# Retention, ELU block and gated block on one core: a first pass in 256-token groups, score banks of their own, earlier loads, and a lag of two

## The chip, the cores and the metric

The kernel runs on one core of a Trainium2 chip. Its engines each have a queue of their own and run in order: PE multiplies matrices into PSUM, DVE (VectorE) and ACT (ScalarE) work on PSUM and SBUF, POOL (GpSimd) works on SBUF alone, and SP (SyncE) issues the transfers. They wait for one another by semaphores. The metric is the device time of one execution in microseconds (us), the median of several runs. The profile is of one execution; PE has two clock levels, 1.2 and 2.4 GHz, and the profile gives the granted one as a share of 2.4 GHz.

## The reference

Three parts follow one another over 2304 tokens (4 batches of 576) with 512 features.

```python
scores = scale * np.matmul(q, k.transpose(0, 1, 3, 2))      # 4 batches, 8 heads, 576 tokens, 64 wide
ret = scores * Dmat                                         # gamma ** (i - j) where i >= j, else 0
attn_out = np.matmul(ret, v)
x = attn_out.transpose(0, 2, 1, 3).reshape(B * S, H * D)    # 2304 x 512
h = x @ w_in                                                # 512 -> 2048
g = np.where(h > 0.0, h, np.exp(np.minimum(h, 0.0)) - 1.0)
x = g @ w_out                                               # 2048 -> 512
gate = 1.0 / (1.0 + np.exp(-(x @ w_gate)))                  # 512 -> 1536
out = gate * (x @ w_val) @ w_out2                           # 1536 -> 512
```

## The kernel before

**Retention** is done in 18 *steps*. A step takes 64 tokens of two batches (X = 0, 1) and all heads, so 128 tokens of the output. `scores` writes K^T Q of the step into PSUM (64x64 matmuls in fp32, each of which stands twice in the trace) and DVE masks it into `a` with `tri` (L192). `outs` is 48 such matmuls (96 in the trace), in three parts: state times Q (32 in the trace, reading `st`), K V for the new state (32), and `a` times V (32). Then DVE adds the new state to `st` (L219); in every second step POOL scales `st` (L222); DVE scales the output out of PSUM (L228, twice); ACT and DVE split it into a high and a low part of `x` (L81, L82). Ahead of a step, POOL scales its V in place (`scale`, L176). All of this uses one PSUM tile `T` of two banks: scores and the new state share its lower half-banks, the outputs its upper ones.

The three parts of `outs` use different rows of the PE array for the same banks. So that the second doesn't overtake the first, the program puts a `nop` on SP that waits for the first 16 matmuls and for which the K V matmuls wait. It stands in SP's queue among the transfers. The transfers (L165 for q and k of two batches and two steps, L169 for k and v of one step, L105 for a weight) share eight semaphores in turn, so each is issued only after the eighth before it has landed, and after the tile it writes has been read for the last time. Steps are loaded two ahead.

**The two dense blocks** take the tokens in five groups, four of 512 and one of 256 (`GS`), and the hidden features in *passes* of two blocks of 128 (`FP`): 8 passes of the ELU block (0 to 7), then 6 of the gated block. A *unit* is one group and one block of features. `up` makes h (12 matmuls: 4 blocks of features times 3, since a product of split numbers is hi·hi + hi·lo + lo·hi); the activation on ACT and DVE gives `e`; ACT and POOL split it into `g` (L81, L82); `down` multiplies `g` by the second weight (12 matmuls) into four PSUM banks `acc`, over both units of a group; `evac` then adds them to `y` (DVE L266). In pass 7 it also splits y for the gated block, on ACT and POOL. The units run with a lag of one: PE does `up` of unit s, then `down` of unit s - 1.

A weight is 512 KB of 64-bit numbers and is turned into two fp32r parts by a *chain* of ACT, DVE and POOL work (L114 to L123, then L81 and L82), which the program spreads over a unit. Four or six chains run in each pass for the next one. The weights of passes 2 and 5 and most of those of passes 8, 10 and 12 lie in a second pool (`w2`), made when the retention's tiles are given up.

Everything is written in the order in which the engines run it. At the start come 18 warm-up matmuls, then 5 steps (`AHEAD`) with the chains of the first four weights between them, then pass 0, in which `retention()` is called ahead of each half of `up` and of `down` and runs half a step each time:

```python
                    retention()
                    up(x_of[g], W["i", f].w, h, (0, 1))
                    first_half()
                    retention()
```

Of the kernel before, what the change touches and what calls it, by code (L numbers as in the profile page):

```python
# [19 lines left out]
NP = H // 2  # L20
# [14 lines left out]
AHEAD = 5  # L35
WARM = 18
# [7 lines left out]
def retention_elu_glu(  # L44
# [22 lines left out]
    ps_acc = ctx.enter_context(tc.tile_pool(name="ps_acc", bufs=4, space=bass.MemoryType.PSUM))  # L67
    ps_h = ctx.enter_context(tc.tile_pool(name="ps_h", bufs=2, space=bass.MemoryType.PSUM))
    ps_t = ctx.enter_context(tc.tile_pool(name="ps_t", bufs=1, space=bass.MemoryType.PSUM))

    acc_bank = lambda: ps_acc.tile([128, 512], F32, tag="acc", name="acc")
# [5 lines left out]
    T = ps_t.tile([128, 2, 512], F32, name="t")  # L77
# [6 lines left out]
    def mm3(out_, wh, wl, xh, xl, start, stop):  # L84

        pe.matmul(out_, wh, xh, start=start, stop=False)  # L86
        pe.matmul(out_, wh, xl, start=False, stop=False)  # L87
        pe.matmul(out_, wl, xh, start=False, stop=stop)  # L88
# [10 lines left out]
    class Weight:  # L99
# [3 lines left out]
        def load(self):  # L103
            self.raw = rpool.tile([128, 2 * DM], I32, tag="raw", name="raw")
            sp.dma_start(out=self.raw, in_=self.src.bitcast(I32))  # L105
# [40 lines left out]
    x_of, y_of, acc, g_of = {}, {}, {}, {}  # L146

    class Step:
# [4 lines left out]
        def __init__(self, n):  # L153
# [4 lines left out]
            self.at = 128 * (n - G0[self.g])  # L158

        def load(self):  # L160
            key = (self.b, self.c)
            if key not in Step.qk:
                Step.qk[key] = [qkpool.tile([128, NP, 2 * C], F32, tag=f"qk{X}", name=f"qk{X}") for X in range(2)]
                for X in range(2):
                    sp.dma_start(out=Step.qk[key][X],  # L165
                                 in_=ain[self.b + X, self.c, :, :, : 2 * C].rearrange("p q x -> q p x"))
            self.kv = kvpool.tile([128, NP, 2 * C], F32, tag="kv", name="kv")
# [5 lines left out]
        def scale(self):  # L173
            v = self.kv[:, :, C:].rearrange("t p (h d) -> t p h d", h=2)
            by = vt[self.s].rearrange("t (p x) -> t p x", x=4)[:, :, 2:4].unsqueeze(3).to_broadcast([128, NP, 2, D])
            pool.tensor_tensor(out=v, in0=v, in1=by, op=ALU.mult)  # L176
# [4 lines left out]
        def scores(self):  # L181
            s = slice(HC * self.s, HC * self.s + HC)
            ks = slice(C + HC * self.s, C + HC * self.s + HC)
            qk = Step.qk[self.b, self.c]
# [119 lines left out]
    with tc.manual_schedule():  # L304
# [38 lines left out]
        def retention():  # L343
# [3 lines left out]
            if n >= NSTEP:  # L347
                return
# [180 lines left out]
```

## Time and profile before

| | us |
|---|---|
| median of 3 runs (lowest, highest) | 973.81 (972.59, 974.82) |
| the profiled execution | 977.69 |
| its span, first to last instruction | 975.6 |
| PE busy | 924.0 |
| DVE, ACT, POOL busy | 458.4, 360.8, 331.0 |

A matmul's end is modelled, so busy PE time overlaps; how fast PE goes is read from the distance of two starts. What a stage costs is read from stretches cut where a pass begins.

### The profile page before, as it was taken

How to read it: one execution, taken by the hardware profiler on the slowest of the kernel's cores; microseconds unless marked ns; L12 is line 12 of the kernel's file. 1: busy time of each engine (PE TensorE's matmuls, PEld its weight loads, DVE VectorE, ACT ScalarE, POOL GpSimd, SP SyncE). 2: the span in 40 equal slices, each digit the busy share in tenths (PEclk: the TensorE clock that was granted, in tenths of full speed). 3: DMA queues.
4: the chain of work that ended last, by engine and by line, in shares of the span. 5: the costliest groups of instructions: out<-in, count | busy, mean ns of one | idle time of the engine just before them, and what ended most of it. 6: DMA issues, size and time to landing. Idle time of an engine off the chain costs nothing.

```text
span 975.6 us, 15096 instructions
## 1 busy us (share of the span) xinstructions
PE 924.0 (95%) x6266; PEld 765.0 (78%) x6266; DVE 458.4 (47%) x740; ACT 360.8 (37%) x633; POOL 331.0 (34%) x261
## 2 busy tenths in 40 slices
PE   5578899999999999999989999999999999999997
PEld 4456778888888887888767888888888888888886
DVE  2554453454555555545666244355355354353222
ACT  1123346454544444444575234223223223222111
POOL 1424333343333334333676222233232232322111
PEclk8689999999999999999998999999999999999999
DMA  7466641110101111111121111111111110100124
GB/s 230 136 180 175 186 153 44 44 44 27 46 36 44 44 44 44 44 44 44 44 64 44 44 44 44 44 44 44 43 44 37 50 44 27 54 7 1 44 48 103
DMA packets 33859, 61.58 MB, mean 63 GB/s; under 512 B 3200, under 2 KB 22656, under 8 KB 33792
## 3 DMA queue, kind: packets, MB, share of 16 engines
q1 hardware_dynamic: 33792, 60.63, 21.0%
q8 instruction: 49, 0.80, 0.4%
q14 instruction: 18, 0.15, 0.0%
HBM read 55.90 MB, written 4.72 MB: 62 GB/s over the span
## 4 chain that ended last, share of the span: by engine, by line
PE 79%; DVE 6%; ACT 5%; POOL 3%; issue 2%; DMA 2%; SPq 0%; DVEq 0%; ACTq 0%; POOLq 0%
PE acc L87 10%; PE h L86 10%; PE h L88 10%; PE acc L88 10%; PE h L87 10%; PE acc L86 10%; PE t L86 5%; PE t L87 5%; PE t L88 5%; PE t L179 4%; POOL g L82 3%; DVE e L244 2%; DMA kv<-in_ain 2%; ACT e L242 1%; ACT e L241 1%
## 5 line engine op out<-in xcount | busy, mean ns | idle before, releaser
L82 POOL TENSOR_TENSOR g<-e,g 128x512 fp32r<-128x512 f32 (+1 forms) x140 | 189.4, 1353 | 549.8 <-ACT g L81 526.4
L86 PE MATMUL h<-x,w 128*128 128x512 f32 (+1 forms) x560 | 209.3, 374 | 0.0
L87 PE MATMUL h<-x,w 128*128 128x512 f32 (+1 forms) x560 | 207.7, 371 | 0.0
L88 PE MATMUL h<-x,w 128*128 128x512 f32 (+1 forms) x560 | 207.7, 371 | 0.0
L81 ACT CAST g<-e 128x512 fp32r<-128x512 f32 (+1 forms) x140 | 81.0, 579 | 220.1 <-DVE e L279 155.2
L279 DVE TENSOR_TENSOR e<-e,t 128x512 f32<-128x512 f32 (+1 forms) x60 | 38.1, 634 | 242.5 <-PE t L88 242.5
L87 PE MATMUL acc<-g,w 128*128 128x512 f32 (+1 forms) x320 | 121.3, 379 | 7.4 <-POOL g L82 7.4
L244 DVE SCALAR_TENSOR_TENSOR e<-e,h 128x512 f32<-128x512 f32 (+1 forms) x80 | 50.7, 633 | 154.9 <-ACT e L242 154.9
L86 PE MATMUL acc<-g,w 128*128 128x512 f32 (+1 forms) x320 | 120.7, 377 | 0.8 <-ACT g L81 0.8
L86 PEld LDWEIGHTS h<-x,w 128*128 128x128 f32 x560 | 105.8, 189 | 19.6
L88 PEld LDWEIGHTS h<-x,w 128*128 128x128 f32 x560 | 105.9, 189 | 18.9
L87 PEld LDWEIGHTS h<-x,w 128*128 128x128 f32 x560 | 105.9, 189 | 18.7
L88 PE MATMUL acc<-g,w 128*128 128x512 f32 (+1 forms) x320 | 119.3, 373 | 0.0
L82 POOL TENSOR_TENSOR w<-t,w 128x512 fp32r<-128x512 f32 x68 | 90.4, 1329 | 21.0 <-ACT w L81 20.9
L86 PE MATMUL t<-x,w 128*128 128x512 f32 (+1 forms) x240 | 88.7, 370 | 0.0
L87 PE MATMUL t<-x,w 128*128 128x512 f32 (+1 forms) x240 | 88.7, 370 | 0.0
L88 PE MATMUL t<-x,w 128*128 128x512 f32 (+1 forms) x240 | 88.5, 369 | 0.0
L274 ACT ACTIVATE e<-h 128x512 f32<-128x512 f32 (+1 forms) x60 | 33.3, 555 | 142.5 <-PE h L88 142.5
L86 PE MATMUL acc<-w,g 128*128 128x512 f32 x216 | 84.6, 392 | 0.0
L88 PE MATMUL acc<-w,g 128*128 128x512 f32 x216 | 84.6, 392 | 0.0
L87 PE MATMUL acc<-w,g 128*128 128x512 f32 x216 | 84.6, 391 | 0.0
L241 ACT ACTIVATE e<-h 128x512 f32<-128x512 f32 (+1 forms) x80 | 44.3, 554 | 99.8 <-PE h L88 97.4
(50 smaller groups left out, 1240.2 us busy)
## 6 DMA issues: line engine op xcount, KB each, us to landing
qk<-in_ain SPq DMA_DIRECT2D x20, 512.0 KB, 7.0
kv<-in_ain SPq DMA_DIRECT2D x36, 256.0 KB, 5.6
raw<-in_w_in SPq DMA_DIRECT2D x16, 512.0 KB, 3.6
raw<-in_w_out SPq DMA_DIRECT2D x16, 512.0 KB, 3.6
raw<-in_w_gate SPq DMA_DIRECT2D x12, 512.0 KB, 3.5
raw<-in_w_val SPq DMA_DIRECT2D x12, 512.0 KB, 3.5
raw<-in_w_o SPq DMA_DIRECT2D x12, 512.0 KB, 3.5
out<-y SPq DMA_DIRECT2D x36, 128.0 KB, 2.4
```

Source lines behind the costliest of these rows:

```text
L81: act.copy(hi, src)
L82: lo_engine.tensor_tensor(out=lo, in0=src, in1=hi.bitcast(F32), op=ALU.subtract)
L86: pe.matmul(out_, wh, xh, start=start, stop=False)
L87: pe.matmul(out_, wh, xl, start=False, stop=False)
L88: pe.matmul(out_, wl, xh, start=False, stop=stop)
L179: return pe.matmul(out_, w, x, start=start, stop=True, skip_group_check=True)
L241: act.activation(out=e, in_=h, func=AF.Relu, scale=-1.0)
L242: act.activation(out=e, in_=e, func=AF.Exp, scale=-1.0)
L244: dve.scalar_tensor_tensor(out=e, in0=e, scalar=-1.0, in1=h, op0=ALU.add, op1=ALU.max)
L274: act.activation(out=e, in_=h, func=AF.Sigmoid)
L279: dve.tensor_tensor(out=e, in0=e, in1=v, op=ALU.mult)
```

## The change

- Pass 0 takes the tokens in nine groups of 256 (`N0`), so it has 18 units with matmuls of 256 columns. Their four sums share two banks (`acc0`, `acc1`).
- Scores get a tile `ts` of two banks, outputs and new state another, `to`. `block(n)` issues the `outs` of step n, then the loads, then the scores of step n + 1 in one stretch; then the state, the scaling (one DVE instruction for both X), the mask and the split. One block goes ahead of each unit of pass 0; two (`AHEAD`) and the first scores go ahead of unit 0. The first step of a batch pair multiplies no state and copies the new one.
- Loads run five steps ahead. The additional tiles are the `y` tiles of later groups, as long as they are not written.
- The constants are loaded from ACT's queue. At the start, the chains of the first two weights follow the blocks whole instead of in pieces.
- `down` of unit s - 2 (`LAG`) follows `up` of unit s; `g` has four tiles instead of three, and a raw weight two instead of three. `evac` comes after all of `down` rather than after each half.
- In pass 7 half of the low parts of the split of y are made on DVE.

```diff
-AHEAD = 5
-WARM = 18
+N0 = 256
+AHEAD = 2
+LAG = 2
+WARM = 24
...
-    rpool = ctx.enter_context(tc.tile_pool(name="raw", bufs=3))
+    rpool = ctx.enter_context(tc.tile_pool(name="raw", bufs=2))
...
-    gpool = ctx.enter_context(tc.tile_pool(name="g", bufs=3))
+    gpool = ctx.enter_context(tc.tile_pool(name="g", bufs=LAG + 2))
...
+            if self.final:
                 x = x_of["b", g]
-                split(x[:, 0, e, :], x[:, 1, e, :], y, pool)
...
+                split(x[:, 0, e, :], x[:, 1, e, :], y, dve if e % 2 else pool)
...
+        for m in range(5, NSTEP):
+            loads_at.setdefault(m - 2 if m == NSTEP - 1 else m - 5, []).append(steps[m].load_kv)
...
+        def block(n):
+
+            if n >= 0:
                 steps[n].outs()
-                if n + 2 < NSTEP:
-                    steps[n + 2].load()
...
+            for load in loads_at.get(n, []):
+                load()
+            if n + 1 < NSTEP:
+                steps[n + 1].scores()
+            if n >= 0:
+                steps[n].state()
+                steps[n].x_scaled()
+            if n + 1 < NSTEP:
+                steps[n + 1].causal()
+            if n + 2 < NSTEP:
+                steps[n + 2].scale()
+            if n >= 0:
+                steps[n].x_low()
...
+        block(-1)
+        for n in range(AHEAD):
+            block(n)
+            for _ in weights[2 * n].chain():
+                pass
...
+        ff = [FF("a", 0, j // 2, f, passes[0][1], j % 2 * N0, N0) for j in range(NT // N0) for f in passes[0][1]]
...
+            if s < begins[1] and s + AHEAD < NSTEP:
+                block(s + AHEAD)
+            if s < len(ff):
+                ff[s].ups(stage, s)
...
+            if s >= LAG:
+                ff[s - LAG].downs(stage)
```

**Where it moves instructions.** Three places matter below. The first is PE within pass 0. Before, six dense matmuls of 512 columns stand between the last matmuls of `outs` (read from `kv` and `a`) and the scores of the next step:

```order
511 L179 MATMUL t<-kv 64x64 x16
512 L179 MATMUL t<-a,kv 64x64 x16
513 L86 MATMUL acc<-g,w 128x512
514 L87 MATMUL acc<-g,w 128x512
515 L88 MATMUL acc<-g,w 128x512
...
519 L179 MATMUL t<-qk_1454 64x64 x2
520 L179 MATMUL t<-qk_1455 64x64 x2
```

After, the scores follow at once, and then a whole unit of 256 columns (12 matmuls of `up`, 12 of `down`) stands ahead of the next step:

```order
585 L189 MATMUL to<-y_110 64x64 x16
586 L189 MATMUL to<-a,y_110 64x64 x16
587 L189 MATMUL ts<-qk_1513 64x64 x2
588 L189 MATMUL ts<-qk_1514 64x64 x2
...
595 L84 MATMUL h<-x_114,w 128x256
596 L85 MATMUL h<-x_114,w 128x256
```

The second is SP's queue at the start. Before, q and k (`qk`), `kv` and weights of the first steps, with eight transfers of constants among them:

```order
3 L169 DMA kv<-in_ain 64x4x256 x2
4 L328 DMA vt_102<-in_csmall 64x16 x2
5 L328 DMA vt_103<-in_csmall 64x16 x2
6 L331 DMA tri<-in_csmall 64x64 x2
7 L332 DMA cq_sb<-in_cq 128x512
8 L333 DMA cs_sb<-in_csmall 128x20
9 L105 DMA raw<-in_w_in 128x1024
10 L169 DMA kv<-in_ain 64x4x256 x2
```

After, twenty transfers of steps 0 to 4 and of four weights stand there (rows 1 to 14; `y_107` to `y_110` are the borrowed tiles), and row 15 is the load of step 5, which follows `outs` of step 0; the `nop` of step 1 (not printed) comes behind row 15, that of step 2 behind row 18:

```order
11 L179 DMA y_109<-in_ain 64x4x256 x2
12 L103 DMA y_107<-in_w_out 128x1024
13 L168 DMA y_108<-in_ain 128x4x256 x2
14 L179 DMA y_110<-in_ain 64x4x256 x2
15 L179 DMA kv<-in_ain 64x4x256 x2
16 L168 DMA qk_313<-in_ain 128x4x256
17 L168 DMA qk_314<-in_ain 128x4x256
18 L179 DMA kv<-in_ain 64x4x256 x2
```

The third is PE at the short group of a later pass (here pass 1). Before, `down` behind the short `up` (`h_2327`) reads `g_2303`, which is made from the h of the unit just before it (`h_2284`):

```order
L88 MATMUL h_2284<-x3_109,w_1795 128x512
L86 MATMUL acc_2310<-g_2262,w_1199 128x512
...
L86 MATMUL h_2327<-x4_110,w_814 128x256
...
L86 MATMUL acc_2310<-g_2303,w_1917 128x512
L87 MATMUL acc_2310<-g_2303,w_1917 128x512
```

After, `down` at that place reads `g_2460`, made one unit earlier than `h_2486`, whose own g is read only a unit later:

```order
L86 MATMUL h_2486<-x3_114,w_1580 128x512
L84 MATMUL acc_2465<-g_2418,w_2033 128x512
...
L84 MATMUL h_2525<-x4_115,w_804 128x256
...
L84 MATMUL acc_2549<-g_2460,w_1138 128x512
L85 MATMUL acc_2549<-g_2460,w_1138 128x512
```

## Rows read from the trace of the kernel before

**Rows 1.** Busy time, clock and DMA of six stages (stretch, length, engines, clock share, DMA share, GB/s).

```profile
0.00:53.22 53.22, 27.96 (x690) 24.72 (x690) 23.34 (x41) 10.84 (x17) 13.60 (x16) 0.72 0.65 191
53.22:157.78 104.56, 91.08 (x1801) 73.00 (x1797) 50.83 (x91) 39.64 (x71) 38.04 (x34) 0.96 0.56 155
157.78:463.26 305.48, 302.34 (x1443) 250.25 (x1441) 157.90 (x273) 146.48 (x256) 111.98 (x84) 1.00 0.13 42
463.26:521.32 58.06, 53.45 (x243) 43.38 (x241) 39.37 (x55) 36.23 (x64) 40.05 (x31) 0.94 0.18 55
521.32:970.13 448.81, 448.81 (x2102) 373.64 (x2100) 185.91 (x283) 127.61 (x225) 127.34 (x97) 1.00 0.14 42
970.13:975.58 5.45, 0.39 (x2) 0.00 (x0) 1.10 (x2) 0.00 (x0) 0.00 (x0) 0.74 0.42 96
```

**Rows 2.** PE's waits up to 53.2 us (in total, times, longest).

```profile
PE t L179 <- DVE a L192: 13.9, 5, 5.4
```

**Rows 3.** Transfers by kind (count, KB each, median us to landing).

```profile
qk<-in_ain SPq DMA_DIRECT2D x20, 512.0 KB, 7.0
kv<-in_ain SPq DMA_DIRECT2D x36, 256.0 KB, 5.6
raw<-in_w_in SPq DMA_DIRECT2D x16, 512.0 KB, 3.6
```

**Rows 4.** Two stretches with the transfer engines nearly full, columns as in rows 1.

```profile
10.00:22.50 12.50, 7.28 (x214) 7.04 (x218) 4.92 (x10) 3.59 (x6) 1.05 (x1) 0.78 0.99 292
65.00:80.00 15.00, 9.66 (x206) 7.70 (x208) 7.20 (x13) 4.04 (x7) 5.76 (x5) 0.95 0.96 242
```

**Rows 5.** PE's timeline in pass 0 around the scores (start, length).

```profile
102.01 0.39 PE L88 MATMUL h<-x,w 128*128 128x512 f32 x1
102.38 0.69 PE L179 MATMUL t<-qk 64*64 64x64 f32 x32
103.00 0.50 PE L86 MATMUL acc<-g,w 128*128 128x512 f32 x1
```

**Rows 6.** The chain that ended last, at `outs` of one step (start, us).

```profile
105.51 2.08 PE t L179 x94
```

**Rows 7.** One unit of pass 0 with its two steps, columns as in rows 1.

```profile
110.81:123.60 12.79, 11.93 (x284) 9.33 (x281) 5.63 (x12) 4.04 (x8) 5.46 (x5) 1.00 0.52 150
```

**Rows 8.** PE's timeline in pass 1: starts 24 matmuls apart (512 columns), then 12 (256).

```profile
184.31 0.39 PE L86 MATMUL h<-x,w 128*128 128x512 f32 x1
...
189.75 0.39 PE L86 MATMUL h<-x,w 128*128 128x512 f32 x1
...
205.39 0.28 PE L86 MATMUL h<-x,w 128*128 128x256 f32 x1
...
206.82 0.28 PE L86 MATMUL acc<-g,w 128*128 128x256 f32 x1
```

**Rows 9.** The same in pass 2, weights in the second pool: starts 24 apart.

```profile
235.46 0.40 PE L86 MATMUL h<-x,w 128*128 128x512 f32 x1
...
241.08 0.40 PE L86 MATMUL h<-x,w 128*128 128x512 f32 x1
```

**Rows 10.** Groups by line and shape: DVE's add and POOL's scaling of the state.

```profile
L219 DVE TENSOR_TENSOR st<-st,t 128x512 f32<-128x512 f32 x16 | 11.0, 686 | 33.7 <-PE t L179 33.6
...
L222 POOL TENSOR_TENSOR st<-st,cs_sb 128x512 f32<-128x512 f32 x8 | 8.9, 1117 | 1.6 <-DVE st L219 1.5
```

**Rows 11.** PE's waits from 158 to 463 us.

```profile
PE acc L87 <- POOL g L82: 3.1, 12, 0.3
```

**Rows 12.** PE's waits from 463 to 522 us (pass 7).

```profile
PE acc L87 <- POOL g L82: 3.8, 4, 2.3
```

**Rows 13.** POOL's timeline in pass 7: low parts of one group's split.

```profile
505.63 5.03 POOL L82 TENSOR_TENSOR x<-y,x 128x512 fp32r<-128x512 f32 x4 [0.18 <-ACT x L81]
```

**Rows 14.** Busy time at the end of pass 7, columns as in rows 1.

```profile
511.90:518.70 6.80, 5.34 (x14) 4.28 (x15) 5.92 (x9) 2.64 (x5) 3.74 (x5) 0.50 0.26 75
```

**Rows 15.** SP's timeline at the end: stores of the last two groups.

```profile
963.30 9.66 SPq L302 DMA_DIRECT2D out<-y  x12
```

More of the change, by code (lines that the diff above doesn't have):

```diff
@@ L143, in retention_elu_glu @@
                 of_pass[-1].append(W[n, f])
[L146 removed]
+    x_of, y_of, acc = {}, {}, {}
     class Step:
@@ new lines, in state @@
+        def state(self):
+            if self.cc == NS - 1:
+                return
+            new = to[:, :, : NP * D].rearrange("d x (p e) -> d x p e", p=NP)
+            if self.cc:
+                dve.tensor_tensor(out=st, in0=st, in1=new, op=ALU.add)
+            else:
+                dve.tensor_copy(st, new)
+            if self.s:
+                by = cs_sb[:, 4 * NP : 5 * NP].unsqueeze(1).unsqueeze(3).to_broadcast([128, 2, NP, D])
+                pool.tensor_tensor(out=st, in0=st, in1=by, op=ALU.mult)
@@ L318, in retention_elu_glu @@
             x_of[g] = x_tile(g)
-        pool.memset(st, 0.0)
-        warm = cpool.tile([128, 256], BF16, name="warm")
         dve.memset(warm, 0.0)
-        steps[0].load()
-        for s in range(2):
-            for X in range(2):
-                r = slice(64 * X, 64 * X + 64)
-                sp.dma_start(out=vt[s][r], in_=csmall[64 * s : 64 * s + 64, : 4 * NP])
         for X in range(2):
             r = slice(64 * X, 64 * X + 64)
-            sp.dma_start(out=tri[r], in_=csmall[r, 5 * NP + 64 * X : 5 * NP + 64 * X + HC])
@@ L334, in retention_elu_glu @@
         weights[0].load()
-        steps[1].load()
+        steps[1].load_kv()
         weights[2].load()
-        weights[1].load()
-        for i in range(WARM):
-            pe.matmul(T[:, 0, :256], warm[:, :128], warm, start=True, stop=True)
-        phase = 0
-        def retention():
-            nonlocal phase
-            n, second = divmod(phase, 2)
-            if n >= NSTEP:
-                return
-            phase += 1
-            if not second:
-                steps[n].scores()
-                if n + 1 < NSTEP:
-                    steps[n + 1].scale()
-            else:
-                steps[n].outs()
-                if n + 2 < NSTEP:
-                    steps[n + 2].load()
@@ L359, in first_weights @@
-        def first_weights():
-            for i in (0, 2, 1, 3):
-                if i == 3:
-                    weights[3].load()
-                yield from weights[i].chain()
-        steps[0].scale()
-        chain = first_weights()
-        for _ in range(2 * AHEAD):
-            retention()
-            for _ in range(2):
-                next(chain, None)
-        for _ in chain:
-            pass
-        ff = []
-        for P, (kind, fs) in enumerate(passes):
-            for g in range(NG):
-                for f in fs:
-                    ff.append((kind, P, g, f, f == fs[0], f == fs[-1]))
@@ L380, in retention_elu_glu @@
-        per = NG * FP
-        conv = {}
+        steps[2].load_qk()
+        steps[2].load_kv()
+        weights[1].load(raws[:, 0, :])
+        steps[3].load_kv()
+        weights[3].load(raws[:, 1, :])
+        steps[4].load_qk()
+        steps[4].load_kv()
+        for i in range(WARM):
+            pe.matmul(ts[:, 0, :256], warm[:, :128], warm, start=True, stop=True)
+        loads_at = {}
+        for m in range(5, NSTEP):
+            loads_at.setdefault(m - 2 if m == NSTEP - 1 else m - 5, []).append(steps[m].load_kv)
+            if steps[m].s == 0:
+                i = steps[m].i
+                of = 0 if i < 3 else i - 3 if i < 8 else i - 2
+                if i >= 3:
+                    last = max(k.n for k in steps if k.i == of)
+                    loads_at.setdefault(max(m - 5, last), []).insert(0, steps[m].load_qk)
@@ L452, in retention_elu_glu @@
+            stage()
+            if halves is not None:
+                next(halves)
+            halves = chain
+            if s < begins[1] and s + AHEAD < NSTEP:
+                block(s + AHEAD)
+            if s < len(ff):
+                ff[s].ups(stage, s)
             else:
                 stage()
-            prev = mine
-            if s == per - 1:
-                assert phase == 2 * NSTEP
+                stage()
+            for w in loads.get(s, []):
+                w.load()
```

323 lines of the change are left out of this document (168 added, 155 removed).

## The prediction

> **What bounds the kernel now.** I read the span by stages first [rows 1]; the stages are cut where PE starts the first dense matmul of a pass. The reader should see four kinds of stage. The gated block (448.81 us) has PE busy all of its time at full clock, so nothing in the order can shorten it. Passes 1 to 6 (305.48 us) are nearly as full. Pass 0 (104.56 us) and the start ahead of it (53.22 us) are not: the start has PE busy for 27.96 us at a mean clock share of 0.72, with no dense matmul in it. Pass 7 (58.06 us) is longer than a sixth of the six passes before it (50.9 us).
>
> How far each stage is from full follows from the distance of two starts. In pass 1, 24 matmuls of 512 columns take 189.75 - 184.31 = 5.44 us, 0.2267 each, and 12 of 256 columns 1.43 us, 0.1192 each [rows 8]. In pass 2, with weights in the second pool, it is 5.62 / 24 = 0.2342 [rows 9]; the tiles of weights stay where they are, so I carry this over. A pass of the ELU block has 192 wide and 48 narrow matmuls: 43.53 + 5.72 = 49.25 us, or 50.69 us from the second pool. Passes 1 to 6 need 4 x 49.25 + 2 x 50.69 = 298.4 us, and take 305.48: 7.1 us are waits. PE's waits there name them: 12 times, twice a pass, for the low part of `g` on POOL [rows 11] (the row's 3.1 us counts idle time only; the modelled ends hide the rest). Pass 7 wastes 58.06 - 49.25 = 8.8 us: PE waits up to 2.3 us for POOL [rows 12], which had four low parts of x (5.03 us) in its queue ahead of `g` [rows 13], and the clock then falls to its lower level, 1.2 GHz, for 6.8 us [rows 14].
>
> In the start, PE waits for the mask and the DVE work around it [rows 2]: the steps are a chain from engine to engine.
>
> **The start.** After the change unit 0 needs the blocks of steps 0 to 2 and the scores of step 3, instead of five steps and the scores of the sixth. What decides is SP's queue. The `nop` of step 2 stands behind the load of step 6, and the second half of that waits for the eighth transfer before it, the last of q and k for step 4. Up to there lie three pairs of q and k (6 x 0.524 MB), four kv (8 x 0.262), four weights (4 x 0.524) [rows 3] and 0.3 MB of constants: 7.6 MB. With its engines full in the early stretch the transfer side moved 292 GB/s [rows 4]; from 2.5 us on that is 28.8 us. Then 0.7 us for the issue, the last two thirds of `outs` (2/3 x 2.08 = 1.4 us at full clock [rows 6], double at half; I take 2.0), and the scores (0.62 to 1.2): unit 0 starts at about 33 us, not 53.2. Bounds: at 242 GB/s, the other full stretch [rows 4], 37.5 us. If the `nop` held up nothing, kv of step 2 (5.0 MB, 19.6 us) and about 6 us of chain behind it would give 26.
>
> **Pass 0.** A block on PE costs 2.08 us for `outs` [rows 6], 0.62 for the scores (102.38 to 103.00), 0.14 for going over to 64x64 (from 102.01 + 0.23 to 102.38), and about 0.1 for going back [rows 5]: 2.94 us. A unit adds 24 x 0.1192 = 2.86 [rows 8]. So a full unit takes 5.80 us with one step in it; before, two steps and one wide unit, the same work, took 12.79, so 6.40 for a step [rows 7]. The sum: unit 0 has only `up`, partly at the lower clock, 2.2; unit 1 a block and `up`, 5.5; units 2 to 15, 14 x 5.80 = 81.2; units 16 and 17 without a block 5.7; less 2.5 for matmuls that don't exist (a step without state at the second pair's start, two steps without new state, no scores after the last); and 2 us for stalls. That makes 94.1 us. Pass 1 begins at 127.1 instead of 157.8, with one narrow `down` (1.43 us) more left over: **29.3 us won**.
>
> Is PE the bound there? From the end of `outs` to the next one PE has 0.62 + 2.86 + 0.24 = 3.7 us of other work. In that time the state must be added (0.69) and in every second step scaled by POOL (1.12) [rows 10]: 1.8 us, and what `a` needs, two more DVE instructions of the same size, may come 1.4 us later still. DVE has four such instructions and a narrow activation in a step (3.2 us), and in six of the 18 units four more of a chain, at that size 2.7 us: that one unit is full, its neighbours not, so I take 2 us for all. The narrow matmuls themselves cost 432 x 0.1192 - 49.25 = 2.2 us, contained in the sum. The Trainium skill, "TensorE: Matmul & The Clock Gate", section "Back-to-back issue gap", puts an isolated gap at N/2.4 + 2.5 ns, 109 ns for 256 and 216 for 512 columns; the trace has 119 and 227, and by the page the split of pass 0 would cost 0.5 us instead of 2.2.
>
> Loading needs about 1.2 MB for a step (q, k, v and a share of weights), 207 GB/s at 5.8 us, against 242 to 292 at full [rows 4]. With some 3.2 transfers to a step, the eighth before is 14 us old, and landing takes 5.6 to 7.0 [rows 3]. So SP shouldn't hold up a `nop` once the first queue is worked off. The constants on ACT's queue cost ACT some 4 us in which it has no work.
>
> **Lag of two, passes 1 to 6.** The stall falls where one `up` or `down` of the pair ahead of a `down` is short: the g it needs is one unit old. With one more unit (2.9 us or more) in between, those waits go: **7 us** (bounds 0 and 7.1). The evacuation now follows the whole `down`, but the next `down` starts an `up` later, so no bank is late.
>
> **Pass 7.** Two of a group's four low parts move from POOL to DVE, 2.5 us of 5.03 [rows 13], and g gets a unit of slack. Of POOL's 40.05 us in the stage [rows 1] some 30 remain; DVE's 39.37 become about 45 of the 50 that PE needs, so DVE is the tight one. If PE doesn't stop, the clock doesn't fall either. I take **7.5 us** of the 8.8 (bounds 0 and 8.8).
>
> **End.** The stores of the last wide group start an `up` later (2.9 us). SP needs 9.66 us for 12 stores with a gap between groups [rows 15], about 0.62 each: eight take 5.0, and their first now comes 3.9 us ahead of PE's end, so the last four start 1.1 us after that end instead of 0.2. Less the last wait for g (0.3), which goes: **0.7 us lost** (bounds 0 and 1.5).
>
> **Sum.** -29.3 - 7 - 7.5 + 0.7 = -43.1 us. The profiled span of 975.6 becomes 932.5, its execution's 977.69 about 934.6. This execution is 3.9 us above the median of the timed runs, so I take the difference from the median: 973.81 - 43.1, **931 us**.
>
> **Rivals.**
> - *A step is bound by its chain, not by PE*: DVE and POOL with chains in between, as before. At the 6.40 us of before [rows 7] 15 blocks cost 9 us more, at 7 us 18 more: 940 to 949. For it: DVE's and POOL's load above. Against: before, scores, state and outputs shared one tile, which set the order of every wait; it's now two. Chance 0.20.
> - *The lag frees little*: DVE is late in pass 7 in POOL's stead, or the short `up` still meets a late g: 7 to 14 us more, 938 to 945. Chance 0.10.
> - *Narrow matmuls are bound by loading weights.* Loads average 250.25 / 1441 = 0.174 us [rows 1]; at that spacing pass 0 grows by 432 x 0.055 = 24 us: 955. Against it stand 0.1192 us in a row of twelve [rows 8]. Chance 0.02. The Trainium skill, "TensorE: Matmul & The Clock Gate", section "Part 3: Packing small matmuls — row/col tiling", says that a load overlaps a running matmul only where the row groups differ; that would give more than 0.28 us a matmul and 1001 us, and the trace disagrees with 0.119.
> - *Slower: SP's queue.* If the eighth transfer before isn't landed when a block's loads are issued, the `nop`, and with it PE, waits for a landing in each step: 2.08 + 7.0 + 0.6 = 9.7 us a step [rows 3, 6], 58 us more, 989 us. The point from which it decides is 5.80 + 43/15 = 8.7 us a step, that is under 138 GB/s; the full stretches are far above [rows 4]. Chance 0.04.
> - *No change*: 0.02, as sums of these.
>
> **How the numbers follow.** My forecast has 0.62, with 921 to 938 as its own range: the start's bounds (-7, +4.5), no stalls or four (-2, +2), pass 7 (-1.3). The range of 919 to 949 takes in the chain and the lag cases and leaves out the last three and the fringes. Within 0.2% (about 1.9 us, what a measurement here can tell from no change) I put 0.02, slower 0.04, faster 0.94.
>
> **What would show it.** The first dense matmul near 33 us, and SP waiting there for transfers; outputs and scores as one piece of about 2.7 us every 5.8 us, with 0.119 us between dense starts; pass 1 near 127 us; no wait for POOL's `g` in passes 1 to 6; no fall of the clock at the end of pass 7; an unchanged gated block; a tail about 1 us longer. I am wrong if units of pass 0 take over 6.4 us, with PE waiting for DVE or the `nop`, or if the 512-column spacing changes.

## The result, and the profile after

The changed kernel takes 944.36 us (median of 4 runs, 939.90 to 948.02) against 973.2 for the kernel before on the same chip: a ratio of 0.9706, 95% interval 0.9656 to 0.9756. Run again later, it took 945.83 us, 0.9707 (0.9685 to 0.9729). So it is 28.8 us faster, where 43 were forecast. The profiled execution took 939.9 us with a span of 937.9; it is the fastest of its four, and that of the second set (944.61) shows where the difference lies, so both are used below.

The stages, cut as in [rows 1] (stretch, length, engines, clock share, DMA share, GB/s):

```profile
0.00:36.41 36.41, 18.18 (x408) 15.58 (x408) 12.56 (x20) 7.19 (x11) 8.05 (x12) 0.66 1.00 268
36.41:128.74 92.33, 88.54 (x2202) 85.18 (x2201) 63.98 (x103) 47.63 (x113) 43.37 (x44) 0.99 0.61 174
128.74:427.47 298.73, 298.73 (x1442) 250.70 (x1441) 160.41 (x272) 148.23 (x263) 101.76 (x85) 1.00 0.14 43
427.47:481.01 53.54, 50.49 (x242) 41.52 (x240) 38.95 (x58) 32.02 (x57) 26.54 (x21) 1.00 0.16 50
481.01:931.28 450.27, 450.10 (x2112) 375.00 (x2111) 188.31 (x291) 130.09 (x232) 117.41 (x97) 1.00 0.15 43
931.28:937.90 6.62, 0.39 (x2) 0.00 (x0) 1.12 (x2) 0.00 (x0) 0.00 (x0) 0.91 0.69 160
```

| stage | before | forecast | after | after, second set |
|---|---|---|---|---|
| unit 0 begins | 53.22 | 33 | 36.41 | 39.09 |
| pass 0 | 104.56 | 94.1 | 92.33 | 94.56 |
| pass 1 begins | 157.78 | 127.1 | 128.74 | 133.65 |
| passes 1 to 6 | 305.48 | 298.4 | 298.73 | 298.73 |
| pass 7 | 58.06 | 50.6 | 53.54 | 53.54 |
| gated block | 448.81 | 450.2 | 450.27 | 450.26 |
| rest | 5.45 | 6.2 | 6.62 | 6.6 |

The gated block holds the 1.43 us of a narrow `down` more that the forecast counted in pass 0. From pass 1 on the two executions agree within 0.1 us; what differs lies ahead of it. The first is the earliest of eight traces with this start: in the others, of the changed kernel and of versions that leave the start alone, pass 1 begins at 132.2 to 136.7 us.

What PE waits for, over the whole run (us in total, times, longest):

```profile
PE to L189 <- issue: 11.2, 2, 10.9
PE to L189 <- POOL kv L186: 3.7, 1, 3.7
PE to L189 <- POOL st L248: 2.7, 2, 1.6
PE acc L84 <- DVE y L343: 2.0, 2, 1.2
PE ts L189 <- issue: 1.9, 1, 1.9
...
PE acc L84 <- ACT g L79: 1.0, 1, 1.0
```

POOL's `g`, twice a pass in [rows 11] and four times in pass 7 [rows 12], is gone. The 10.9 us, for which the profile names no releaser ("issue"), are read as the wait of step 1 for SP's `nop`: the K V matmuls that wait for it go on at 26.50, just after SP ends the issue ahead of it (24.07 + 2.27):

```profile
24.07 2.27 SPq L179 DMA_DIRECT2D kv<-in_ain  x2
26.50 1.13 PE L189 MATMUL to<-kv 64*64 64x64 f32 x32 [10.94 <-issue]
```

What ended last at unit 0's start is the chain below (start, us). It is the one forecast: the last transfer of q and k for step 4 lands at 31.25, SP then issues the second half of step 6 (1.76), and 3.3 us of outputs and scores follow.

```profile
9.19 10.61 DMA qk<-in_ain
19.82 11.43 DMA y<-in_ain
31.26 1.76 SPq L179
33.13 1.33 PE to L189 x37
```

From 2.5 us to that landing the transfer engines moved 286 GB/s, so 8.2 MB (columns as in the stages):

```profile
2.50:31.25 28.75, 12.39 (x291) 10.68 (x290) 8.92 (x13) 5.05 (x8) 6.30 (x6) 0.66 1.06 286
```

A full unit of pass 0 with its step (the columns of the stages; [rows 7] answers to it) takes 5.55 us with PE busy throughout:

```profile
87.65:93.20 5.55, 5.55 (x158) 5.35 (x153) 3.07 (x6) 3.85 (x10) 0.89 (x2) 1.00 0.40 104
```

Pass 7 wastes 4.3 us of its 53.54. Here is DVE in it (start, us, line, operation, idle time before), then PE at the same place:

```profile
459.31 1.28 DVE L343 TENSOR_TENSOR y<-y,acc 128x512 f32<-128x512 f32 x2
461.28 1.34 DVE L80 TENSOR_TENSOR x<-y,x 128x512 fp32r<-128x512 f32 x1 [0.69 <-ACT x L79]
462.54 1.27 DVE L343 TENSOR_TENSOR y<-y,acc 128x512 f32<-128x512 f32 x2
464.50 1.29 DVE L80 TENSOR_TENSOR x<-y,x 128x512 fp32r<-128x512 f32 x1 [0.69 <-ACT x L79]
```

```profile
461.73 0.39 PE L86 MATMUL acc<-g,w 128*128 128x512 f32 x1
463.27 0.50 PE L84 MATMUL acc<-g,w 128*128 128x512 f32 x1 [1.16 <-DVE y L343]
```

The four adds that empty the sums are torn apart: DVE waits 0.69 us for ACT's high part and spends 1.34 on a low part before the third add. The third bank is free only at 463.2, and the next `down` stands.

### The profile page after: what moved, and what is told of

Read it like the earlier page. It is cut to its first block, busy times and chain, and to the rows that moved or that the text cites. A ratio compares the mean times of both kernels' runs of the same rounds, so it can differ in the third digit from the quotient of the medians.

```text
span 937.9 us, 15400 instructions
## 1 busy us (share of the span) xinstructions
PE 906.4 (97%) x6400; PEld 768.0 (82%) x6400; DVE 465.3 (50%) x740; ACT 365.2 (39%) x673; POOL 297.1 (32%) x256
## 4 chain that ended last, share of the span: by engine, by line
PE 91%; DMA 3%; DVE 2%; ACT 2%; issue 1%; SPq 0%; POOL 0%; ACTq 0%; DVEq 0%; POOLq 0%
PE h L84 12%; PE h L85 12%; PE h L86 12%; PE acc L84 12%; PE acc L85 12%; PE acc L86 12%; PE tv L84 5%; PE tv L85 5%; PE tv L86 5%; PE to L189 3%; DMA y<-in_ain 1%; DMA qk<-in_ain 1%; PE ts L189 1%; ACT x L79 1%; DMA vt<-in_csmall 1%
## 5 line engine op out<-in xcount | busy, mean ns | idle before, releaser
L80 POOL TENSOR_TENSOR g<-e,g 128x512 fp32r<-128x512 f32 (+1 forms) x148 | 167.2, 1130 | 573.3 <-ACT g L79 540.1
L84 PE MATMUL h<-x,w 128*128 128x512 f32 (+1 forms) x592 | 215.1, 363 | 0.0
L85 PE MATMUL h<-x,w 128*128 128x512 f32 (+1 forms) x592 | 213.2, 360 | 0.0
L86 PE MATMUL h<-x,w 128*128 128x512 f32 (+1 forms) x592 | 213.1, 360 | 0.0
L300 DVE TENSOR_TENSOR e<-e,tv 128x512 f32<-128x512 f32 (+1 forms) x60 | 38.1, 634 | 230.7 <-PE tv L86 230.5
L84 PEld LDWEIGHTS h<-x,w 128*128 128x128 f32 x592 | 112.1, 189 | 18.8
L84 PE MATMUL acc<-g,w 128*128 128x512 f32 (+1 forms) x352 | 124.3, 353 | 3.0 <-DVE y L343 2.0
L85 PEld LDWEIGHTS h<-x,w 128*128 128x128 f32 x592 | 112.2, 190 | 17.7
L86 PEld LDWEIGHTS h<-x,w 128*128 128x128 f32 x592 | 112.3, 190 | 17.5
L85 PE MATMUL acc<-g,w 128*128 128x512 f32 (+1 forms) x352 | 123.9, 352 | 0.0
L86 PE MATMUL acc<-g,w 128*128 128x512 f32 (+1 forms) x352 | 123.8, 352 | 0.0
L84 PE MATMUL tv<-x,w 128*128 128x512 f32 (+1 forms) x240 | 88.7, 369 | 0.2 <-DVE e L300 0.2
L85 PE MATMUL tv<-x,w 128*128 128x512 f32 (+1 forms) x240 | 88.7, 370 | 0.0
L86 PE MATMUL tv<-x,w 128*128 128x512 f32 (+1 forms) x240 | 88.6, 369 | 0.0
```

Source lines behind the costliest of these rows:

```text
L80: lo_engine.tensor_tensor(out=lo, in0=src, in1=hi.bitcast(F32), op=ALU.subtract)
L84: pe.matmul(out_, wh, xh, start=start, stop=False, skip_group_check=shared)
L85: pe.matmul(out_, wh, xl, start=False, stop=False, skip_group_check=shared)
L86: pe.matmul(out_, wl, xh, start=False, stop=stop, skip_group_check=shared)
L300: dve.tensor_tensor(out=e, in0=e, in1=v, op=ALU.mult)
```

## The experiments

Eleven kernels, each a changed version of the changed kernel, and the changed kernel once more. "Pass 1 begins" stands for start and pass 0 together.

**Lag of one** (`LAG = 1`).

> The changed kernel with a lag of one again, the rest kept (g has three tiles). Theory: the lag took the waits out of passes 1 to 6 and part of them out of pass 7, and pass 0 does not need it since a block of retention lies between a unit and its g. So passes 1 to 6 go from 298.7 back to about 305.5 us, with PE waiting for the low part of g twice a pass; pass 7 from 53.5 to 56 or more; pass 0 stays within 3 us of 92.3; in all 8 to 13 us longer than the changed kernel, a ratio of 0.978 to 0.985 to the kernel before. Rival: the waits went because the sums are now taken out after the whole down; then passes 1 to 6 stay at 299 us and the ratio at 0.971.

Measured: ratio 0.9723 (0.9698 to 0.9749), 948.63 us. Passes 1 to 6 take 299.88 us, 1.15 more, not 7; pass 7 takes 56.62 (3.1 more), and the clock falls in it again (0.97). Pass 0 takes 98.27, 6 us more and not within 3, with a stop of 4.5 us of the kind taken up below among it. At 3 to 4 us the whole missed the 8 to 13. So the waits of [rows 11] were gone without the lag. The rival's number came out, but its reason wasn't tested by this. The POOL rows of passes 1 to 6 gave another: the low part of `g` takes 1.30 us here and took 1.52 on average before. Behind that stands where the chain's pieces lie among DVE's work, which the change moves too, so that was taken apart.

**Order of the chain, lag of one and of two.**

```diff
-                stage()
                 dve.scalar_tensor_tensor(out=e, in0=e, scalar=-1.0, in1=h, op0=ALU.add, op1=ALU.max)
...
             self.finish(e)
+            if self.kind == "a":
+                stage()
```

> The changed kernel with a lag of one, and in units of the ELU block the third piece of a weight's chain (DVE's add) back behind the split of g, where the kernel before has it; so DVE's last piece (the one that joins sign and exponent, reading raw and t) again comes a good half microsecond later. Theory, new after the first four runs: the 7 us of waits in passes 1 to 6 of the kernel before came from this order, since the last piece then runs beside POOL's low part of g, which takes 1.74 us beside it and 1.30 otherwise; the change took them away by the order, not by the lag. Then passes 1 to 6 take 304 to 306 us here, with POOL's low part at 1.74 us for the 24 units with a chain, against 299.9 with a lag of one and the new order. Rival: something else of the change did it (the sums taken out after the whole down, the tiles of raw); then passes 1 to 6 stay near 300.

> The same order of the chain as in the run just before, with the lag of two. If the lag hides a late g, as I predicted, passes 1 to 6 stay at 298.7 us although POOL's low part takes 1.74 us again; then lag and order are each enough for the 7 us. If the lag hides nothing, they take 304 us or more.

Measured, passes 1 to 6 of each profiled execution:

| | lag of one | lag of two |
|---|---|---|
| order of before | 304.66 | 300.13 |
| order of the change | 299.88 | 298.73 |

The row of the old order is one execution each; the eight traces in which lag, order and weight pools are as in the change all take 298.70 to 298.73, so differences of 1 us are clear here. The stages themselves, lag of one in the old and the new order, then lag of two in the old:

```profile
134.51:439.17 304.66, 301.80 (x1442) 250.28 (x1441) 156.93 (x273) 146.72 (x256) 112.11 (x84) 1.00 0.14 42
136.70:436.58 299.88, 299.88 (x1442) 250.19 (x1441) 155.97 (x273) 146.15 (x256) 101.27 (x84) 1.00 0.14 43
136.68:436.81 300.13, 299.92 (x1443) 250.94 (x1441) 160.79 (x272) 148.78 (x263) 112.28 (x85) 1.00 0.14 43
```

Each alone gives 4.5 to 4.8 us, both together 5.9: either hides most of the same waits. The evacuation behind the whole `down`, the rival of the first run, doesn't take them away: with it, a lag of one and the old order, 304.66 us are left of the 305.48 of the kernel before. The two rows of POOL below are from passes 1 to 6 with a lag of one, first in the order of before, then in that of the change (busy us, mean ns of one):

```profile
L80 POOL TENSOR_TENSOR g<-e,g 128x512 fp32r<-128x512 f32 x48 | 73.2, 1525 | 166.7 <-ACT g L79 147.6 <-PE acc L86 19.1
```

```profile
L80 POOL TENSOR_TENSOR g<-e,g 128x512 fp32r<-128x512 f32 x48 | 62.4, 1299 | 172.8 <-ACT g L79 146.8 <-PE acc L86 26.0
```

The mean of 1525 ns mixes two kinds. Of the 48, the 24 that overlap DVE's last piece of the chain (L121, inputs `raw` and `t`, both in SBUF) take 1.74 to 1.76 us, the others 1.28 to 1.32, also beside DVE's adds from PSUM. Such a pair, in the order of before:

```profile
177.14 0.69 DVE L121 SCALAR_TENSOR_TENSOR t<-raw,t 128x512 uint32<-128x512 uint32 x1
```

```profile
177.24 1.74 POOL L80 TENSOR_TENSOR g<-e,g 128x512 fp32r<-128x512 f32 x1 [4.13 <-ACT g L79]
```

In the order of the change L121 runs beside ACT's copy, ahead of POOL's low part, and the two don't meet. The Trainium skill, "SBUF — State Buffer", section "Who interferes with whom", says that a DVE instruction with two SBUF inputs contends with a GpSimd instruction that reads SBUF, and one with at most one SBUF input outside the two-port modes doesn't. The trace agrees on which pairs collide: 1.74 us for POOL beside L121, 1.28 to 1.32 beside the adds from PSUM. In the pair above DVE starts 0.10 us ahead; POOL loses 0.44 us to an overlap of 0.59, DVE nothing.

**Adds ahead of the splits in pass 7.**

```diff
             if self.last:
                 for i, a in enumerate(sums):
                     (self.evac_a if self.kind == "a" else self.evac_b)(i, a)
+                if self.kind == "a" and self.final:
+                    for e in range(KB):
+                        self.split_x(e)
```

> In pass 7 the four adds of a group's sums to y come first on DVE, and the four splits behind them, instead of add and split in turn. Theory: the 4.3 us that pass 7 still wastes (53.54 against 49.25) come from sums that are taken out late, since DVE's low part of x stands between the second and the third add and waits for ACT there. Then pass 7 falls to 50 to 51.5 us, and no wait of PE for y is left there; about 3 us in all. Rival: g itself is late, because ACT, POOL and DVE have the splits ahead of it; then pass 7 stays at 53 to 54 us and the wait only changes its name to g.

Measured: 0.9634 (0.9609 to 0.9660), 940.16 us. Pass 7 falls to 49.79 us, a little below what was expected, and no wait of PE is left in it. By stages the edit is worth 4.2 us, 3.7 here and 0.4 in the pass behind it; the ratio's 7, taken on another chip, hold the spread of start and pass 0 as well.

```profile
433.18:482.97 49.79, 49.79 (x241) 41.76 (x240) 39.86 (x58) 31.33 (x55) 26.55 (x20) 1.00 0.18 53
```

**All low parts of pass 7 on POOL again** (`pool` for `dve if e % 2 else pool`).

> In pass 7 all four low parts of the split are made on POOL again; adds and splits stay in turn. My prediction's theory: half of them on DVE is worth a good part of pass 7, since four on POOL (5.0 us) stand ahead of g; then pass 7 goes from 53.5 to 55 us or more, with PE waiting for g. Rival, from the run with the adds first: DVE's in-order low part is what makes the sums late, so without it pass 7 is shorter, 50 to 52.5 us, and the lag of two lets POOL's queue pass.

Measured: pass 7 takes 51.05 us, the rival's value; one execution, 940.92 us. With the lag of two, half of the split on DVE costs 2.5 us where adds and splits alternate; it is no gain. In the changed kernel seven of the eight wide low parts that DVE makes in this split take 1.28 to 1.40 us, and one 0.69. Each of the seven starts 0.44 to 0.56 us behind a low part of POOL, which takes its 1.29 to 1.30 all the same; the one starts 0.09 us ahead of POOL's, and then POOL loses. Here are POOL beside DVE's 461.28 above, and then the one:

```profile
460.78 1.29 POOL L80 TENSOR_TENSOR x<-y,x 128x512 fp32r<-128x512 f32 x1
...
474.00 0.69 DVE L80 TENSOR_TENSOR x<-y,x 128x512 fp32r<-128x512 f32 x1 [0.69 <-ACT x L79]
474.09 1.74 POOL L80 TENSOR_TENSOR x<-y,x 128x512 fp32r<-128x512 f32 x1
```

So the split shared out between the two sets them side by side, and whichever starts second is the slower one.

**Loads of the start in another order.**

```diff
-        weights[1].load(raws[:, 0, :])
-        steps[3].load_kv()
-        weights[3].load(raws[:, 1, :])
-        steps[4].load_qk()
-        steps[4].load_kv()
...
-        loads_at = {}
+        loads_at = {1: [lambda: weights[1].load(raws[:, 0, :]), steps[3].load_kv,
+                        lambda: weights[3].load(raws[:, 1, :]), steps[4].load_qk],
+                    2: [steps[4].load_kv]}
         for m in range(5, NSTEP):
-            loads_at.setdefault(m - 2 if m == NSTEP - 1 else m - 5, []).append(steps[m].load_kv)
+            loads_at.setdefault(m - 2 if m == NSTEP - 1 else max(m - 4, 2) + (m == 6), []).append(steps[m].load_kv)
```

> The same loads, but SP's queue in another order at the start: the transfers of w_out's two blocks, of kv 3, of q and k 4 now stand behind the nop of step 1, kv 4 and 5 behind that of step 2, and so on one or two steps later than in the changed kernel, from step 7 on four steps ahead. Theory: unit 0 was held to 36.4 us by the nop of steps 1 and 2, which stood behind issues that waited for the eighth transfer before them; now they are not, and the data of kv 2 land at about 22 us, so unit 0 begins at 26 to 29 us, 7 to 10 us earlier; pass 0 may give 1 to 4 us of it back where q, k and v of steps 4 to 6 land late. The whole becomes 4 to 9 us shorter, a ratio of 0.961 to 0.967. Rival: the transfers as such bind, 8 to 9 MB in the first 36 us, so the nop is late because the data are; then unit 0 may begin earlier but pass 1 begins at 128 to 129 us as now, ratio 0.971. A second rival: four steps ahead is too little, and PE waits for landings in pass 0, slower than the changed kernel.

Measured: 0.9657 (0.9634 to 0.9681), 943.14 us: by the ratio some 5 us less than the changed kernel, by the medians 1 to 3, on different chips. The `nop` is no longer waited for up to unit 0, but that begins at 30.54, not 26 to 29. Up to there PE waits for POOL's scaling of the state, which stands in POOL's queue behind the scaling of V of step 2:

```profile
PE to L189 <- POOL st L248: 4.9, 1, 4.9
```

Pass 1 begins at 128.26 in an execution of 939.2 us: most of the gain at the start is given back in pass 0, 97.72 us. The ratio is in the range of the theory, the stage is the rival's. The rival's reason (the transfers bind) doesn't hold in pass 0: PE waits there 5.4 us for "issue", 2.1 for POOL's scaling of the state, and for no landing.

**PE kept busy in the wait of step 1.**

```diff
                         swept = after(sp.nop(), ins)
+                if self.n == 1:
+                    hb = h_bank()
+                    for _ in range(80):
+                        pe.matmul(hb[:, :256], warm[:, :128], warm, start=True, stop=True)
```

> 80 matmuls of 256 columns on zeros are put ahead of the K V matmuls of step 1, where PE waits some 11 us at the start of the changed kernel; they write a bank of h that is read by nothing. Theory on the clock: the granted clock falls to its lower level at 18.5 us because PE stands, and is at it until 39 us; with PE at work from 15.6 to some 24 us it falls later or not at all, the blocks of steps 1 and 2 and the up of unit 0 (3.9 us of work at full clock) go at 2.4 GHz, and pass 1 begins 1 to 4 us earlier, with less spread between runs; ratio 0.966 to 0.970. Rival: the transfers set it all, pass 1 begins as before at 129 to 136 us, ratio 0.971. Second question: in all five traces so far PE stops at the same place of its stream, ahead of its 987th matmul, for 1.9 to 4.4 us, waiting for nothing that the profile shows. If that hangs on the count of its instructions (they have to be fetched, beside the loads), the stop stays at that count and so falls 80 matmuls earlier in the program, before the scores of step 5; if it hangs on what the program does there, it stays in the scores of step 5, at the 1067th matmul.

Measured: 0.9709 (0.9683 to 0.9735), 947.62 us: no gain, though the clock stays at its upper level from 15.9 to 33.0 us, where the changed kernel's is at the lower one from 18.5 to 39.0 (here it falls at 33.0, up to 39.8). Unit 0 begins at 37.97 and pass 1 at 132.86, as in the traces without the 80 matmuls: PE still waits for the `nop` of step 2, 3.2 us, where the two traces of the changed kernel have 0.8 and 2.1. On the second question neither outcome came as it was put: no stop stands ahead of the 987th matmul, none ahead of the 1067th, and the new ones of over 0.9 us stand ahead of the 732nd and the 1751st. It is answered by the count all the same: the stops of the changed kernel and its versions lie at a count of 222 and whole multiples of some 127 above it, whatever the program does there. The trace of the changed kernel names a queue for instructions (packets, MB, share of the engines):

```profile
q8 instruction: 50, 0.82, 0.4%
```

Its packets are of 16,384 bytes. Beside such stops, worked out from the traces' records in us (after and after_again are the two traces of the changed kernel, e_warm is this one, e_best that of the three edits at the end):

```
kernel       matmuls  last start  packet   goes on  packet to going on
after            986       58.96    58.42    61.04   2.62
after_again      986       61.36    61.13    63.99   2.86
e_warm           731       48.70    47.90    50.86   2.96
e_best           604       38.84    39.10    41.84   2.74
e_best           986       55.32    54.43    57.33   2.90
e_best          1496       79.15    78.39    81.30   2.91
```

In the thirteen traces of the changed kernel and its versions 31 gaps of over 0.9 us between the starts of two matmuls stand at these counts; in 30 of them PE goes on 2.3 to 3.0 us after a packet began. So PE stands there, by counts and packets, because its next instructions aren't in yet. The Trainium skill, "Runtime: NRT & Kernel Launch", section "Instruction fetch mechanics", says that instructions come in 16 KiB blocks and that crossing a block is mostly hidden. The size agrees; hidden it is not in pass 0 of this kernel.

**One tile for scores, outputs and state** (`ts = to`, `state()` ahead of the scores).

> The scores share the tile of the outputs and of the new state again (one tile of two banks), so the add of the new state goes ahead of the scores and PE waits for it between outputs and scores of each step; all else as in the changed kernel. Theory: the banks of their own are worth that wait, DVE's add of 0.69 us and two handovers, 1.0 to 1.8 us in each of 15 steps of pass 0: 15 to 27 us longer, ratio 0.986 to 0.998. Rival: pass 0 is held by loads and by fetching anyway, and the wait only takes their place: under 8 us longer, ratio under 0.979.

Measured: 0.9810 (0.9777 to 0.9843), 956.42 us, some 10 us longer by the ratio: between the theory's 15 to 27 and the rival's 8. A full unit takes 6.60 us, 1.05 more, the lower end of the theory's price for a step, and PE waits for DVE's add:

```profile
PE to L189 <- DVE st L243: 13.8, 14, 2.4
```

These 6.60 us are no less than the 6.40 of a step in the kernel before [rows 7]: in this order the 256-token groups alone make no step shorter, the banks do.

**Loads two steps ahead** (`m - 2` for `m - 5`).

> Steps 5 to 17 are loaded two steps ahead as in the kernel before, the first five at the start as in the changed kernel. Theory: a step of pass 0 takes 5.55 us, and q and k are needed by the scores one step after the issue, while they land in 6 to 8 us; so PE waits 1 to 3 us in every second step, or at the nop behind the issues, and pass 0 takes 5 to 20 us longer (98 to 112 us), ratio 0.976 to 0.992; unit 0 begins earlier, at about 30 us, since no load of step 5 or 6 stands ahead of the nop. Rival: loads five ahead are not what pass 0 lives on; then pass 1 begins at 128 to 134 us as now or earlier, ratio 0.966 to 0.971.

Measured: 0.9751 (0.9725 to 0.9777), 949.76 us, 4 us longer than the changed kernel beside it; unit 0 begins at 34.70, pass 0 takes 105.35, 10.8 more than there. The 30 for unit 0 was wrong: at the start PE waits 8.8 us for POOL's scaling of V of step 2, whose data land at 23.05. The other waits are of the kind expected, for landings and for POOL behind them:

```profile
PE to L189 <- POOL y L186: 8.8, 1, 8.8
PE to L189 <- POOL st L248: 7.1, 6, 2.3
...
PE ts L189 <- DMA qk<-in_ain: 2.7, 3, 1.4
```

**32 bytes of padding ahead of the second pool** (a tile `[128, 8]` F32 in a pool of its own, opened before `w2`).

> 32 bytes of padding ahead of the second pool of weights, so that its tiles begin at a multiple of 64 bytes as those of the first pool do (before: 32 bytes behind one); nothing else. Theory: the 0.2342 us between matmuls with weights from the second pool, against 0.2267, come from that address. Then passes 2 and 5 take 49.2 to 49.3 us each instead of 50.7, and the units of passes 8, 10 and 12 that read it fall likewise; in all 5 to 7 us shorter than the changed kernel, ratio 0.964 to 0.966. Rival: the distance has another cause (the region of SBUF, or the neighbours of the pool); then nothing changes, 0.971.

Measured: 0.9666 (0.9636 to 0.9695), 943.17 us. Pass 2 falls from 50.65 to 50.38 us and pass 10 from 75.18 to 74.99, not to the 49.3 of the first pool: the address modulo 64 isn't the cause, or only a small part of it, and the rest stays open. Stage by stage it is worth some 1 us; the ratio can't tell that.

**The changed kernel once more, and three edits together.**

```diff
+        loads_at = {1: [lambda: weights[1].load(raws[:, 0, :]), steps[3].load_kv,
+                        lambda: weights[3].load(raws[:, 1, :]), steps[4].load_qk, steps[4].load_kv]}
...
+            if n in (1, 2, 3):
+                steps[n + 1].scale()
-            if n + 2 < NSTEP:
+            if n + 2 < NSTEP and n not in (0, 1, 2):
                 steps[n + 2].scale()
```

(beside the adds ahead of the splits and the padding)

> The changed kernel itself, unaltered, on the chip of the next three runs, as the base for them. Both theories: a ratio near 0.971; passes 1 to 6, pass 7 and the gated block within 0.3 us of the first trace (298.7, 53.5, 450.3), pass 1 beginning anywhere from 128 to 137 us, so that the spread between its runs lies in the start and pass 0 alone; and a stop ahead of the 987th matmul, as in all the traces that have the same stream there.

> Three edits together: in pass 7 the adds ahead of the splits; the loads of the start in an order in which no nop stands behind a transfer that is not needed there anyway (kv 4 now ahead of the nop of step 2, steps 5 and later behind it), with POOL scaling V of steps 2 to 4 behind the state of the step before instead of ahead of it; 32 bytes of padding for the second pool. Theory: pass 7 falls to 49.8 us (-3.7), the padding gives 0.6, and unit 0 begins at 27 to 31 us with fewer waits for POOL behind it, so that pass 1 begins at 122 to 128 us: in all 7 to 11 us less than the changed kernel beside it, ratio 0.960 to 0.963. Rival: the transfers bind the steps up to the sixth (two runs so far say so), so pass 1 begins at 128 us or later as ever; then only 4 to 5 us, ratio 0.965 to 0.967.

Measured: 0.9707 (0.9685 to 0.9729) for the changed kernel and 0.9647 (0.9621 to 0.9673), 938.85 us, for the three edits: faster than both kernels by the intervals. The ratio lies between the two forecasts, the 7.0 us to the changed kernel beside it at the lower end of the theory; pass 1 is where the rival has it. Unit 0 begins at 28.59, pass 7 takes 49.76, but pass 1 begins only at 133.10. Here are the stages of start and pass 0 with the three edits, and what PE waits for in pass 0:

```profile
0.00:28.59 28.59, 17.50 (x408) 14.33 (x408) 12.20 (x20) 7.18 (x11) 7.91 (x11) 0.79 0.98 272
28.59:133.10 104.51, 92.92 (x2202) 88.64 (x2201) 64.82 (x103) 47.72 (x113) 42.89 (x44) 0.96 0.63 173
```

```profile
PE to L189 <- issue: 8.2, 5, 2.8
PE ts L189 <- issue: 1.8, 1, 1.8
PE acc L85 <- issue: 1.4, 1, 1.4
PE h L85 <- DVE x L262: 0.2, 1, 0.2
```

No transfer and, but for 0.2 us, no engine holds PE up in pass 0 now: 11.4 us are "issue", and six gaps of over 0.9 us at the counts above make 12.4 us (two more, 3.7 us, lie in the start). One of the six, in the middle of 32 matmuls that need nothing new, and the stages of that gap and of a later one:

```profile
38.83 0.23 PE L189 MATMUL to<-y 64*64 64x64 f32 x2
41.84 0.51 PE L189 MATMUL to<-y 64*64 64x64 f32 x18 [2.78 <-issue]
```

```profile
39.10:41.80 2.70, 0.00 (x0) 0.00 (x0) 2.63 (x6) 0.00 (x0) 0.91 (x1) 1.00 1.10 241
...
100.90:103.30 2.40, 1.08 (x10) 0.99 (x9) 2.13 (x4) 1.43 (x4) 2.40 (x2) 1.00 0.04 9
```

The changed kernel has one such gap of over 0.9 us (2.1 and 2.6 us in its two traces), the order of loads further up five, this one eight. Pass 0 takes 10.0 to 12.2 us more than in those two traces, and 9 of them are the longer wait for "issue"; behind two of the stops the clock is also at its lower level for 3.4 us each (57.8 to 61.2 and 81.7 to 85.1). So what takes back the 8 to 10 us won at the start is in the main the supply of instructions, not the transfers. Why PE runs out at one count and not at the next, and more often after an earlier start, isn't settled: full transfer engines aren't needed, since the DMA share between packet and going on is from 0.04 to 1.10 in the eight. Fewer PE instructions for a step were not tried. The three edits are no faster than the adds ahead of the splits alone (0.9634, another chip).

Not taken apart are the steps ahead of unit 0 (`AHEAD`), the narrow groups of pass 0 and the constants on ACT's queue. Of the 24 to 29 us by which pass 1 begins earlier, the banks account for some 10 and the early loads for some 4; the rest, 10 to 15 us, isn't shared out among these.

## Why the prediction was right or wrong

The direction, the place and most mechanisms were right, and one term, pass 7, was not. The sum was 14.3 us too high: 43.1 against 28.8. The measured 944.36 is outside the 921 to 938 of the forecast itself, and inside the wider range because that takes in two rivals (940 to 949 and 938 to 945). The first of them, steps bound by their chain, is refuted: 5.55 us for a full unit, not 6.40 or more. The second has its first condition fulfilled, DVE late in pass 7 in POOL's stead, at 3.0 us and not 7 to 14. That the time meets their numbers is luck.

Profile against profile the change wins 37.8 us (977.69 to 939.9). Of the 5.3 that are missing there, 1.6 lie ahead of pass 1, 3.0 in pass 7 and the rest in passes 1 to 6 and the end. The other 9 lie in which executions were profiled: the one before took 4.5 us more than the median of 973.2, the one after 4.5 less than the median of 944.36.

- **The start** was decided as forecast, by the `nop` of step 2 behind the load of step 6 behind the eighth transfer. That landed at 31.25, not 28.8. Mis-sized was mainly what moves up to then: 8.2 MB from 2.5 us on, not 7.6, since transfers issued behind it ran beside it; the 286 GB/s are near the 292 taken from [rows 4]. SP's issue took 1.76, not 0.7. Unit 0 came 3.4 us late (6 in the second set). That earlier data wouldn't have helped as much as the bound of 26 says, I didn't see: the order of the loads brought 30.54 and 28.59, and pass 0 took most of it back.
- **Pass 0** was PE-bound as argued, with 5.55 us for a full unit, not 5.80, and 120 ns between narrow matmuls. Its waits were more than the 2 us allowed: for POOL's scaling of the state at unit 1 (1.6 and 2.6 us in the two traces), and for instructions in unit 3 (1.9 and 2.4), of which the working held nothing. That 92.33 is so near to 94.1 is two errors of opposite sign, 14 units at 0.25 us less and some 2 us of waits more. The banks of their own are worth 1.05 us a step, the early loads some 4 us.
- **Passes 1 to 6**: 6.75 us won against 7, and the waits for `g` are gone. That the lag hides a late `g` is shown (300.13 us with POOL at 1.74). That it was the part of the change that did it, is not: the moved piece of the chain takes away 4.8 us alone. I read that wait as "g is one unit old" and didn't ask why POOL took 1.52 us instead of 1.30.
- **Pass 7** is the step that failed: 4.5 us won against 7.5. "No bank is late", argued for passes 1 to 6 and right there, was carried over to pass 7, where the splits stand between the adds on DVE; with the adds first the stage takes 49.79. "2.5 us move from POOL to DVE" was counted as a gain and costs 2.5 us beside the lag. That the clock doesn't fall was right; of the two kernels with a lag of one it falls in one (0.97) and not in the other, whose pass 7 takes 57.56.
- **The end** was 1.17 us longer against 0.7; the gated block is unchanged but for the `down` left over.
- **The base**: the stages of before were those of an execution 3.9 us above the median, and the sum was taken off the median. Where those 3.9 us lay in the kernel before was not looked for. In the changed kernel the second set shows it: 4.9 us more in the span, all of them ahead of pass 1.

## What to carry to other kernels

Where a wait goes away with a change of several parts, run each part alone before crediting one: two that hide the same wait look like either. On an in-order engine, put what frees a bank ahead of what merely uses its result. And a start-up won by earlier data is worth only what the next limit leaves, here the supply of PE's instructions: look for stops at fixed counts of them.

## What the hardware showed unexpectedly

- PE stopped for 1 to 5 us at fixed counts of matmuls, going on in 30 of 31 cases 2.3 to 3.0 us after a 16,384-byte packet of the instruction queue, in and behind blocks of small matmuls, at a DMA share of 0.04 as at 1.10.
- POOL's low part took 1.74 us where it started behind DVE's instruction with two SBUF inputs and 1.30 otherwise, 24 of 24 times in one kernel. Where DVE's started second it was DVE that lost, 1.28 to 1.40 us instead of 0.69, seven of seven times.
- Wide matmuls whose weights lie in the second pool start 0.234 us apart, against 0.227 from the first; 32 bytes of address explain 0.27 of 1.4 us a pass, and the rest is open.
- The two executions of the changed kernel differ by 4.9 us in span, and all of it lies ahead of pass 1; the passes after it agree within 0.1 us. In the eight traces with an unchanged start pass 1 begins at 128.7 to 136.7 us.
